# An FFT filter and a top-128 FFN: input rows laid out by halves on the host, and loaded by SyncE as 112 partitions and one

## The chip, the cores and the metric

One core of a Trainium2 chip runs the program. The time is device microseconds (us) of one execution. TensorE multiplies matrices into PSUM, VectorE and ScalarE work on SBUF and PSUM, GpSimd on SBUF alone, and SyncE (SP) issues DMAs. In the rows of the profile they are PE, DVE, ACT, POOL and SP; ACTq and SPq are the sequencers of ACT and SP, which hand out their instructions, DMA issues among them, in program order.

## What is computed

```
x: (8, 3136, 256) float32;  filt: (1569, 256), complex;  capacity C = 128
y   = irfft(rfft(x, axis=1) * filt, n=3136, axis=1)        # a filter along the sequence
s   = y . w_gate                                           # one score per row
top = the 128 rows of largest score, in each of 8 batches
out = y;  out[top] = y[top] + sigmoid(s[top]) * (relu(y[top] @ w1) @ w2)
```

## The kernel before

The transform of length 3136 = 98 * 32 is done by matmuls in two steps, and so is the way back.

**The work on one batch.** `outer` (by eight chunks of 32 channels) makes the first step of the batch that comes in and the last step of the batch that goes out. In: `fold` (L381) adds and subtracts the two halves of the rows, `amm` (L391) multiplies by the 98-point table, `tout` (L396) transposes into `UU`. A chunk that the plan names in `UNF` has no folds, and its `amm` has twice the matmuls ("plain"). Out: `tin` (L373) transposes from `UU`, `ymm` (L457) multiplies, `yout` (L460) copies from PSUM to `X`, and a store goes out once the four chunks of a half of the channels are done. `inner` (seven steps) does the 32-point part with the filter between: `zmm` (L292), `pmul` on VectorE (L300) and `zout` on ScalarE with `qmul` on GpSimd (L296, L303), `vmm` (L312), `vout` (L316, L320, L322), and the scores, `gate` on VectorE (L328) or `gmul` and `gsum` on GpSimd and ScalarE (L342, L347). `select` finds the 128 rows by counting (L604 on ScalarE, L613 on TensorE), after a trip of the scores through DRAM (`scr`, `R`, both DMAs on SP). While `inner` works on batch t, `outer` takes t-1 out and t+1 in. An FFN on the chosen rows ends the program.

**X** is one buffer for both ways: rows of y that wait for their store, and rows of x of the batch after next, by halves of the channels. A half is loaded when its store has read it, and stored when its chunks are done. A row of x is 256 channels in DRAM, so a half of it is a run of 512 bytes. The 49 rows of a quarter lie in a group of 64 partitions, the first 32 of them in order and the others at every second partition, and the rest of the group is set to zero at the start. A half takes ten DMAs: four on ACT's queue for one group, four on SP's for the other, and two on SP's for the last row of each. There are sixteen such loads in all.

**The order.** Each engine's order is made ahead of the run by a planner in the kernel: steps with a cost, what they read and write, and weights in `PLAN` (`LEAN`, `FOLD`, `UNF` and others). It replays the steps with these costs and always takes the one that could start first, after the weights. In that replay the ACT part of a load costs ACT 1.45, whatever its DMAs wait for:

```python
            op(when, "act", 1.45, lambda: rows_in(b, d, 1, nc.scalar), ["xpad"] if b == 0 else [], keys[1], lat=14.0 if b == 0 else 9.5, bias=bias)
            op(when + .001, "sp", 7.8, lambda: (rows_in(b, d, 0, nc.sync), last_in(b, d)), ["xpad"] if b == 0 else [], keys[0], lat=2.2, bias=bias)
```

On the chip the order within an engine is fixed, and semaphores alone hold it back. 160 warm-up matmuls on zeros (L987) stand first on TensorE.

Of the kernel before, what the change touches and what calls it, by code (L numbers as in the profile page):

```python
# [57 lines left out]
def _place():
    at = np.full(NH, LAST_ROW)
    for a, p, n, step in ROWS:  # L60
        at[a:a + n] = p + step * np.arange(n)
    return at


def _tables(C):
# [83 lines left out]
    TRING=['z', 'm', 'm', 'v', 'v'],
    URING=['v', 'm', 'v', 'z', 'm'],  # L150
# [3 lines left out]
    LEAN=dict(pmul=(-5.347, 0.016), yout=(-17.362, 0.336), turned=(38.666, -0.081), vhi=(-45.057, 1.291), gate=(4.527,  # L154
          1.5), vout=(17.794, -0.003), scatter=(-73.692, -0.615), tout=(-2.383, 0), zout=(14.722, 0.286), qmul=(0.524,
          0.201), tin=(39.462, -0.174), ymm=(-58.554, -0.011), vlo=(-25.455, -0.383), gather=(-40.475, 1.189), turn=(-6.285,
          0.267), xlo=(57.538, 0.676), yadd=(5.004, -0.444), swap=(24.566, 1.128), xhi=(-7.258, 1.5), amm=(8.954, 0.08),
          fold=(-24.881, -0.125), zmm=(-1.426, -0.093), vmm=(-1.82, -0.021), count=(-20.404, -0.51), total=(20.026, 0.066),
          over=(42.03, 0.547)),
    UNF=[[0, 1, 2, 3, 4, 7], [1, 2, 3, 6, 7], [], [0, 1], [0, 1], [0, 3, 4, 6], [0, 5], [0, 1]],  # L160
    GPOOL=[[1, 2, 3, 4, 5], [2, 3], [], [1, 2, 3, 5], [0, 1, 3, 5], [0, 2, 3, 4, 5], [1, 3, 4, 5], [0, 1, 3, 4]],
    JOIN=[[0, 1, 5, 7], [0, 2, 7, 8, 13]],
    IRING=['a'],
# [5 lines left out]
def kernel(  # L169
# [24 lines left out]
    xv = x.rearrange("b (h a g n) d -> b g a h n d", h=2, g=2, n=NG)  # L194
# [15 lines left out]
    X = const.tile([128, 2, NG, D], F32, name="X")  # L210
    XO = X.rearrange("p h n d -> p (h n) d")
# [54 lines left out]
    def inner(T0, TU, b):  # L266
# [5 lines left out]
        for i in range(NQ):  # L272
# [59 lines left out]
            op(t0, "pe", .49 * m + .02, zmm, [u for l in ls for u in row(b, l)] + ["tf"], new=Z, mode=1)  # L332
            op(t0 + 1.0, "act", .15 + .43 * m, zout, [Z], [Z], new=Q)
            op(t0 + 1.0, "dve", .12 + .54 * m, pmul, [Z, *(("fa", k) for k in parts)], new=Y)
            op(t0 + 2.0, "pool", 1.2 * m, qmul, [Q, *(("fb", k) for k in parts)], [Q])
            op(t0 + 4.5, "pe", .88 * m + .02, vmm, [Y, Q, "ti"], new=V, mode=1)
            op(t0 + 6.2, "act", .15 + .43 * m if n > 1 else .3, vout, [V], [V, *(u for l in ls for u in row(b, l))])
# [11 lines left out]
            for ks in ([0, 1], [2, 3]):  # L349
# [821 lines left out]
```

## Time and profile before

| | |
|---|---|
| Three runs | median 587.87 us (586.87 to 590.5) |
| The profiled execution | 585.63 us; its span from first to last instruction 583.8 us |
| Busy share of the span | PE 80%, DVE 70%, POOL 53%, ACT 49% |
| Mean granted TensorE clock | 0.904 of 2.4 GHz |
| DMA | 65.00 MB, mean 111 GB/s |

A busy share is a mean over stages: loading until the first filter product at 52.9 us, batch 0 alone until the first `tin` at 97.6, the first half of an output until its store at 126.2, then eleven half batches until the store at 467.3, and a tail with the last batches and the FFN. What bounds a stage is read from who waits for whom in it.

### The profile page before, as it was taken

Reading aid. Unit: us, or ns where it says so; the run is one execution under the profiler, and the core shown is the slowest. Engines: PE = TensorE matmul, PEld = TensorE weight load, DVE = VectorE, ACT = ScalarE, POOL = GpSimd, SP = SyncE. Lnnn points to the kernel's source line nnn. Section 1 sums busy time; section 2 is a strip of 40 time slices with the busy share of each in tenths; the row PEclk is TensorE's granted clock in tenths of the full one; section 3 lists DMA queues with packets and bytes.
Section 4 is the critical chain, followed back from the end, with each engine's and each line's share of the span. In section 5 each row is a group of like instructions: output and inputs, shape, how many; then the busy total and the mean of one; then the engine's idle time right before and its main releaser. Section 6 shows DMA issues by size and latency. Waiting matters only on the chain.

```text
span 583.8 us, 11344 instructions
## 1 busy us (share of the span) xinstructions
PE 469.4 (80%) x4268; PEld 244.6 (42%) x4268; DVE 411.0 (70%) x988; ACT 284.6 (49%) x612; POOL 312.1 (53%) x202
## 2 busy tenths in 40 slices
PE   9932859899969695997689586969878987869996
PEld 9611424343423242432244132424432354546996
DVE  6443855899949584895579485857859799887542
ACT  1211632586436342784267144545365688936421
POOL 5342976893727151862455053546536389973422
PEclk9985988999979797998989797989978999968999
DMA  9998062328562647045913635180653166513521
GB/s 198 242 230 166 1 111 64 79 61 162 149 112 78 144 113 138 10 136 119 199 21 105 134 113 121 32 190 3 168 84 112 29 185 170 116 44 88 120 70 37
DMA packets 110157, 65.00 MB, mean 111 GB/s; under 512 B 5014, under 2 KB 108438, under 8 KB 109846
## 3 DMA queue, kind: packets, MB, share of 16 engines
q1 hardware_dynamic: 83734, 49.59, 35.3%
q10 hardware_dynamic: 25600, 12.59, 11.5%
q0 software_dynamic: 768, 2.10, 1.2%
q8 instruction: 34, 0.56, 0.4%
q14 instruction: 21, 0.17, 0.1%
HBM read 37.34 MB, written 26.91 MB: 110 GB/s over the span
## 4 chain that ended last, share of the span: by engine, by line
PE 45%; DMA 22%; POOL 8%; DVE 8%; issue 8%; ACT 6%; SPq 1%; ACTq 1%; POOLq 0%; DVEq 0%
DMA X<-in_x_dram 13%; PE py L457 13%; PE pv L312 10%; PE pa L391 8%; DMA out_dram<-X 5%; PE pz L292 5%; POOL q L303 3%; POOL X L429 2%; ACT X L460 2%; PE pa L420 2%; PE pa L898 1%; PE pv L865 1%; DVE X L381 1%; POOL xl L342 1%; DMA fb_sb<-in_fri_dram 1%
## 5 line engine op out<-in xcount | busy, mean ns | idle before, releaser
L303 POOL TENSOR_TENSOR q<-q,fb_sb 128x1024 f32<-128x1024 f32 (+1 forms) x56 | 125.1, 2234 | 171.2 <-ACT q L296 146.9
L457 PE MATMUL py<-t,c_sb 128*98 128x512 f32 x192 | 114.0, 678 | 33.2 <-ACT X L460 32.5
L460 ACT COPY X<-py 98x512 f32<-98x512 f32 x96 | 56.1, 584 | 86.6 <-DMA X<-in_x_dram 46.3
L300 DVE TENSOR_TENSOR y<-pz,fa_sb 128x1024 f32<-128x1024 f32 (+1 forms) x56 | 63.6, 1137 | 44.9 <-ACT q L296 28.4
L391 PE MATMUL pa<-X,c_sb 64*64 64x512 f32 x464 | 89.0, 636 | 1.0 <-DVE UU L396 1.0
L396 DVE STREAM_TRANSPOSE UU<-pa 128x1024 f32<-128x1024 f32 x59 | 73.2, 1241 | 18.9 <-PE pa L391 18.6
L292 PE MATMUL pz<-UU,tf_sb 64*64 64x256 f32 x800 | 62.8, 410 | 26.5 <-DVE y L300 24.6
L373 DVE STREAM_TRANSPOSE t<-UU 128x1024 f32<-128x1024 f32 x64 | 78.8, 1231 | 5.7 <-PE py L457 3.2
L328 DVE SCALAR_TENSOR_TENSOR rj<-pv,wg_sb 128x256 bf16<-128x256 f32 x144 | 60.1, 417 | 27.1 <-ACT UU L320 14.7
L312 PE MATMUL pv<-y,ti_sb 64*64 64x256 f32 x800 | 70.0, 405 | 7.6 <-DVE rj L328 6.2
L296 ACT COPY q<-pz 128x1024 f32<-128x1024 f32 (+1 forms) x56 | 53.2, 949 | 30.8 <-PE pz L292 14.3
L312 PE MATMUL pv<-q,ti_sb 64*64 64x256 f32 x800 | 67.3, 391 | 0.0
L292 PEld LDWEIGHTS pz<-UU,tf_sb 64*64 64x64 f32 x800 | 29.9, 137 | 65.3 <-DVE y L300 30.1
L457 PEld LDWEIGHTS py<-t,c_sb 128*98 128x98 f32 x192 | 25.6, 175 | 70.1 <-ACT X L460 51.5
L342 POOL TENSOR_TENSOR xl<-UU,wg_sb 128x512 f32<-128x512 f32 x28 | 37.7, 1348 | 29.2 <-ACT UU L320 20.8
L391 PE MATMUL pa<-xh,c_sb 64*64 64x512 f32 x160 | 52.2, 716 | 1.1 <-DVE UU L396 0.6
L312 PEld LDWEIGHTS pv<-y,ti_sb 64*64 64x64 f32 x800 | 31.1, 140 | 44.7 <-issue 13.6
L381 POOL TENSOR_TENSOR xh<-X 128x512 f32<-128x512 f32 x28 | 38.1, 1367 | 21.1 <-DMA tf_sb<-in_tf_dram 15.7
L613 PE MATMUL pm<-cr_sb,cnt 128*128 128x16 f32 x56 | 21.8, 389 | 30.1 <-ACT junk L604 29.7
L312 PEld LDWEIGHTS pv<-q,ti_sb 64*64 64x64 f32 x800 | 34.9, 140 | 13.7 <-issue 2.5
L381 POOL TENSOR_TENSOR X<-X 128x512 f32<-128x512 f32 x28 | 38.7, 1389 | 2.1 <-DVE xh L381 1.4
L320 ACT COPY UU<-pv 128x1024 f32<-128x1024 f32 x24 | 24.2, 1007 | 31.4 <-PE pv L312 21.7
(207 smaller groups left out, 745.0 us busy)
## 6 DMA issues: line engine op xcount, KB each, us to landing
out_dram<-X SPq DMA_DIRECT2D x12, 1568.0 KB
X<-in_x_dram ACTq DMA_DIRECT2D x32, 256.0 KB
X<-in_x_dram SPq DMA_DIRECT2D x32, 256.0 KB
out_dram<-X SPq DMA_DIRECT2D x16, 384.0 KB
X<-in_x_dram SPq DMA_DIRECT2D x32, 128.0 KB
X<-in_x_dram ACTq DMA_DIRECT2D x32, 128.0 KB
R<-scr SPq DMA_DIRECT2D x14, 196.0 KB
fb_sb<-in_moe_w_dram SPq DMA_DIRECT2D x2, 1024.0 KB
```

The costliest lines, as they stand in the source:

```text
L292: nc.tensor.matmul(z[o, hi, e], lhsT=tf_sb[p, l], rhs=urow(b, l, 0, D)[p], start=True, stop=True)
L296: nc.scalar.copy(out=wide(q), in_=wide(h["z"]))
L300: nc.vector.tensor_tensor(out=wide(y), in0=wide(h["z"]), in1=filt(fa_sb), op=ALU.mult)
L303: nc.gpsimd.tensor_tensor(out=wide(h["q"]), in0=wide(h["q"]), in1=filt(fb_sb), op=ALU.mult)
L312: nc.tensor.matmul(v[o, j, c], lhsT=ti_at[p, k, 2 * i + e, hi], rhs=y[p, hi, c], start=k == 0, stop=k == 1)
L328: nc.vector.scalar_tensor_tensor(out=rj, in0=h["v"][:, k % 2, k // 2 * D:k // 2 * D + D], scalar=1.0, in1=wg_sb, op0=ALU.mult, op1=ALU.mul ...
L373: nc.vector.transpose(out=h["t"].rearrange("p d (l j) -> p d l j", j=2), in_=uchan(b_out, c))
L381: eng.tensor_tensor(out=area(1) if k else h["f"], in0=area(0), in1=area(1), op=(ALU.add, ALU.subtract)[k])
L391: nc.tensor.matmul(ap[64 * k:64 * k + 64, g].rearrange("p (n d) -> p n d", d=DW), lhsT=todo[k][i][0][p], rhs=todo[k][i][1][p], start=i == ...
L396: nc.vector.transpose(out=uchan(b_in, c), in_=a.rearrange("p (l j) d -> p d l j", j=2))
L457: nc.tensor.matmul(yp[:N1], lhsT=cc["wi"], rhs=half(), start=True, stop=True)
L460: nc.scalar.copy(out=XO[:N1, :, q * CW:(q + 1) * CW], in_=h["y", k][:N1])
```

## The change

The host lays x out anew: by batch, then by half of the channels, then 113 rows of 16 KB (49 rows of one quarter, 15 of zeros, 49 of the other), so that a partition's share of a half is one run in DRAM and, with `X` stored by halves too, one in SBUF. A load is two DMAs on SP's queue, 112 rows and the last one; ACT issues none. The zeroing of `X` at the start falls away, folds take 113 partitions, and `amm` 49 rows of a group. Bytes of a load go from 1568 KB to 1808 KB. A store is still one DMA with runs of 512 bytes in DRAM.

```diff
-    X = const.tile([128, 2, NG, D], F32, name="X")
-    XO = X.rearrange("p h n d -> p (h n) d")
+    X = const.tile([128, 2, 2, NG, HD], F32, name="X")
+    XO = X.rearrange("p x h n d -> p x (h n) d")
...
-                eng.tensor_tensor(out=area(1) if k else h["f"], in0=area(0), in1=area(1), op=(ALU.add, ALU.subtract)[k])
+                eng.tensor_tensor(out=(area(1) if k else h["f"])[:64 + NH], in0=area(0)[:64 + NH], in1=area(1)[:64 + NH],
+                                  op=(ALU.add, ALU.subtract)[k])
...
-                            p = slice(64 * g, 64 * g + 64)
+                            p = slice(64 * g, 64 * g + NH)
...
         if b < B:
-            keys = [[("x", h, c, g) for c in range(h * n, h * n + n)] for g in range(2)]
-            op(when, "act", 1.45, lambda: rows_in(b, d, 1, nc.scalar), ["xpad"] if b == 0 else [], keys[1], lat=14.0 if b == 0 else 9.5, bias=bias)
-            op(when + .001, "sp", 7.8, lambda: (rows_in(b, d, 0, nc.sync), last_in(b, d)), ["xpad"] if b == 0 else [], keys[0], lat=2.2, bias=bias)
+            keys = [("x", h, c, g) for c in range(h * n, h * n + n) for g in range(2)]
+            to = X[:, h].rearrange("p k n d -> p (k n d)")
+
+            def fetch():
+                nc.sync.dma_start(out=to[:112], in_=x[b, h, :112])
+                nc.sync.dma_start(out=to[112:64 + NH], in_=x[b, h, 112:])
+
+            op(when, "sp", 7.2, fetch, [], keys, lat=2.2, bias=bias, tag="load")
...
-    for g, k, e in ((0, 0, "dve"), (0, 1, "pool"), (1, 0, "dve"), (1, 1, "pool")):
-        op(-99.9 + .01 * g, e, 3.5, lambda g=g, k=k, e=e: dict(dve=nc.vector, pool=nc.gpsimd)[e].memset(X[32 + 64 * g:64 + 64 * g, k], 0.0), (), ["xpad"])
...
-    data = {k: np.ascontiguousarray(inputs[k]) for k in ("x", "moe_w_gate", "moe_w1", "moe_w2")}
+    data = {k: np.ascontiguousarray(inputs[k]) for k in ("moe_w_gate", "moe_w1", "moe_w2")}
+    rows_of = np.asarray(inputs["x"]).reshape(B, 2, NH, 2, NG, 2, D // 2).transpose(0, 5, 3, 2, 1, 4, 6)
+    data["x"] = np.zeros((B, 2, 64 + NH, S * D // (4 * NH)), np.float32)
+    data["x"][:, :, :NH], data["x"][:, :, 64:] = rows_of.reshape(B, 2, 2, NH, -1).transpose(2, 0, 1, 3, 4)
```

The planner has new costs for most steps, a replay that charges TensorE's steps double while it takes the clock to be low, and a new table `PLAN`, so that nearly every row of every engine's order moves. Of the table:

```diff
-    AO6=0.179, AO7=0.099, SD=-34.762, WARM=160, FR=17.139, F0=-30.458, G7=-25.255, INV=2,
+    AO6=0.353, AO7=0.107, SD=-30.114, WARM=85, FR=12.002, F0=-84.921, G7=-79.774, INV=2,
```

Counted over the program: warm-up matmuls 160, then 85; folds on VectorE 26, then 36, and on GpSimd 56, then 48; plain chunks 23, then 22 (of batches 2 to 7 12, then 14); score products on VectorE 144, then 152, on GpSimd 28, then 24; the counting steps of one batch more (batch 4) end on ScalarE instead of VectorE.

The order on three places. First ACT at the start of the program, before: loads of batches 0 and 1 (L481) ahead of the copies of the filter table (L966) and the first `zout` (L296).

```order
L481 DMA X<-in_x_dram 32x16x128 x2
L481 DMA X<-in_x_dram 16x16x128 x2
L995 ACTIVATE ti_sb<-ti_sb 32x1664 x2
L481 DMA X<-in_x_dram 32x16x128 x2
L481 DMA X<-in_x_dram 16x16x128 x2
L966 COPY fb_sb<-fb_sb 32x1024 x2
L481 DMA X<-in_x_dram 32x16x128 x2
L481 DMA X<-in_x_dram 16x16x128 x2
L296 COPY q<-pz 128x1024 x2
```

The same place of the changed kernel, where L950 is the copy of the table, L979 the turn of `ti_sb` and L285 `zout`:

```order
L983 ACT_TABLE_LOAD
L983 ACTIVATE sc<-ge 128x1
L950 COPY fb_sb<-fb_sb 32x1024
L979 ACTIVATE ti_sb<-ti_sb 32x1664
L285 COPY q<-pz 128x1024
L979 ACTIVATE ti_sb<-ti_sb 32x1664
```

No DMA stands ahead of the first `zout` now. VectorE at this place, before, up to the first `pmul` (L300):

```order
L396 STREAM_TRANSPOSE UU<-pa 128x32x16x2
L396 STREAM_TRANSPOSE UU<-pz 128x32x16x2
L396 STREAM_TRANSPOSE UU<-pv 128x32x16x2
L396 STREAM_TRANSPOSE UU<-pa 128x32x16x2
L396 STREAM_TRANSPOSE UU<-pz 128x32x16x2
L966 COPY fa_sb<-fa_sb 32x2048
L300 TENSOR_TENSOR y<-pz,fa_sb 128x1024
```

And in the changed kernel, up to its first `pmul` (L289):

```order
L386 STREAM_TRANSPOSE UU<-pa 128x32x16x2
L977 COPY ti_sb<-ti_sb 32x1664
L386 STREAM_TRANSPOSE UU<-pz 128x32x16x2
L962 CAST cr_sb<-UU 128x16
L950 COPY fa_sb<-fa_sb 32x1024
L977 COPY ti_sb<-ti_sb 32x1664
L950 COPY fb_sb<-fb_sb 32x2048
L289 TENSOR_TENSOR y<-pz,fa_sb 128x1024
```

Ahead of them stand six of the eight transposes and all seven folds of batch 0 on VectorE; the turns of `ti_sb`, which stood before all transposes, have come in between.

Second, ACT in the stage of half batches, before: the load between a `yout` (L460) and the next one, with a count of `select` (L604) behind it.

```order
L460 COPY X<-py 98x32x16
L481 DMA X<-in_x_dram 32x16x128 x2
L481 DMA X<-in_x_dram 16x16x128 x2
L460 COPY X<-py 98x32x16
L604 ACTIVATE junk,cnt<-R,c_sb 128x392
L296 COPY q<-pz 128x1024
L322 COPY UU<-pv 128x2x512
```

The changed kernel at the first count of the same batch (L588 is the count, L450 `yout`, L311 `vout`):

```order
L285 COPY q<-pz 128x1024
L311 COPY UU<-pv 128x2x512
L450 COPY X<-py 98x32x16
L588 ACTIVATE junk,cnt<-R,c_sb 128x392
L285 COPY q<-pz 128x1024
L450 COPY X<-py 98x32x16
L611 ACTIVATE ok,J<-pm,c_sb 128x15
L612 ACTIVATE nb<-J,nd 128x1
```

The computing rows are of the same kinds, and nothing that waits for a store is among them.

Third, SP in the same stage, before: a store (L469), its load, the next store, `select`'s trip through DRAM (L548, L574) and that store's load.

```order
L469 DMA out_dram<-X 3136x1x128
L481 DMA X<-in_x_dram 32x16x128 x2
L481 DMA X<-in_x_dram 16x16x128 x2
L486 DMA X<-in_x_dram 2x16x128 x2
L469 DMA out_dram<-X 3136x1x128
L548 DMA scr<-kf 98x2x32
L574 DMA R<-scr 128x1x392 x2
L481 DMA X<-in_x_dram 32x16x128 x2
L481 DMA X<-in_x_dram 16x16x128 x2
L486 DMA X<-in_x_dram 2x16x128 x2
```

And the changed kernel (L459 the store, L475 and L476 the load, L532 and L558 the trip):

```order
L459 DMA out_dram<-X 3136x1x128
L475 DMA X<-in_x_dram 112x4096
L476 DMA X<-in_x_dram 1x4096
L459 DMA out_dram<-X 3136x1x128
L532 DMA scr<-kf 98x2x32
L558 DMA R<-scr 128x1x392 x2
L475 DMA X<-in_x_dram 112x4096
L476 DMA X<-in_x_dram 1x4096
```

SP keeps the sequence store, trip, load; six issues of a load have become two, and four on ACT none.

## Rows read from the trace of the kernel before

**Rows 1.** Waits of ACT: engine, line, waited for, us in total, times, longest.

```profile
ACT X L460 <- DMA X<-in_x_dram: 46.3, 7, 9.9
...
ACT fb_sb L966 <- DMA X<-in_x_dram: 22.3, 1, 22.3
...
ACT Dt L522 <- DMA X<-in_x_dram: 5.9, 1, 5.9
```

**Rows 2.** Waits of PE.

```profile
PE py L457 <- ACT X L460: 32.5, 16, 6.6
PE pm L613 <- ACT junk L604: 29.7, 6, 7.8
PE pz L292 <- DVE y L300: 24.6, 2, 18.3
```

**Rows 3.** Timeline, SP and ACT, 205 to 236 us: start, us, what.

```profile
210.17 0.93 SPq L469 DMA_DIRECT2D out_dram<-X  x1
...
219.28 9.28 ACTq L481 DMA_DIRECT2D X<-in_x_dram  x4
228.60 0.58 ACT L460 COPY X<-py 98x512 f32<-98x512 f32 x1 [9.94 <-DMA X<-in_x_dram]
```

**Rows 4.** Timeline of PE behind it; in brackets its wait and what ended it.

```profile
229.85 0.38 PE L613 MATMUL pm<-cr_sb,cnt 128*128 128x16 f32 x1 [7.23 <-ACT junk L604]
```

**Rows 5.** Stages: length; busy us (count) of PE, PEld, DVE, ACT, POOL; clock, DMA, GB/s.

```profile
52.90:97.60 44.70, 34.35 (x388) 17.79 (x388) 30.95 (x52) 19.94 (x35) 34.28 (x20) 0.82 0.25 47
97.60:126.20 28.60, 25.99 (x254) 11.63 (x250) 24.54 (x59) 15.97 (x28) 25.09 (x18) 1.00 0.32 73
126.20:467.30 341.10, 278.59 (x2373) 116.80 (x2373) 252.68 (x657) 176.52 (x385) 163.60 (x97) 0.90 0.47 108
467.30:583.80 116.50, 96.97 (x825) 73.70 (x817) 80.73 (x207) 64.39 (x159) 71.10 (x54) 0.94 0.39 104
225.70:235.90 10.20, 6.05 (x28) 2.15 (x29) 4.30 (x7) 5.84 (x13) 4.30 (x3) 0.50 0.53 83
```

**Rows 6.** The same for ten stretches without a long gap, and their sum.

```profile
103.70:160.10 56.40, 54.98 (x552) 24.40 (x552) 53.44 (x151) 35.14 (x63) 40.75 (x25) 1.00 0.48 109
...
sum 246.20, PE 239.69 PEld 105.83 DVE 220.94 ACT 145.26 POOL 159.42; mean PE 23.97 PEld 10.58 DVE 22.09 ACT 14.53 POOL 15.94
```

**Rows 7.** Timeline of the start, PE, ACT and DVE.

```profile
1.00 20.15 PE L987 MATMUL pm<-ge 128*64 128x64 f32 x320 [1.00 <-POOL ge L237]
...
31.64 9.83 ACTq L481 DMA_DIRECT2D X<-in_x_dram  x4
...
45.81 5.96 ACTq L481 DMA_DIRECT2D X<-in_x_dram  x4
51.81 1.01 ACT L296 COPY q<-pz 128x1024 f32<-128x1024 f32 x1 [8.21 <-DMA X<-in_x_dram]
...
52.91 1.23 DVE L300 TENSOR_TENSOR y<-pz,fa_sb 128x1024 f32<-128x1024 f32 x1 [16.38 <-issue]
```

**Rows 8.** DMA rates (last column) of three stretches of the start.

```profile
2.00:5.00 3.00, 3.00 (x40) 3.00 (x39) 3.00 (x1) 0.24 (x2) 2.94 (x2) 1.00 0.83 302
...
8.00:14.00 6.00, 6.00 (x107) 6.00 (x106) 3.56 (x3) 0.00 (x0) 0.07 (x1) 1.00 1.10 195
...
20.00:25.00 5.00, 5.00 (x57) 2.45 (x59) 1.87 (x2) 0.00 (x0) 1.25 (x1) 1.00 1.03 276
```

**Rows 9.** Groups of DVE instructions: us busy, mean ns of one.

```profile
L396 DVE STREAM_TRANSPOSE UU<-pa 128x1024 f32<-128x1024 f32 x43 | 53.4, 1243 | 6.4 <-PE pa L391 6.0
...
L328 DVE SCALAR_TENSOR_TENSOR rj<-pv,wg_sb 128x256 bf16<-128x256 f32 x102 | 42.5, 417 | 17.6 <-ACT UU L320 9.2 <-ACT UU L316 4.3 <-ACT UU L322 2.1
...
L966 DVE COPY fb_sb<-fb_sb 32x2048 f32<-32x2048 f32 x2 | 3.4, 1718 | 0.1
```

**Rows 10.** Folds on DVE: ns min/median/max.

```profile
L381 DVE TENSOR_TENSOR xh<-X x13: 651/909/1742, 24.4 to 402.8; 128x512 f32<-128x512 f32 x13
L381 DVE TENSOR_TENSOR X<-X x13: 644/1449/4875, 26.7 to 442.1; 128x512 f32<-128x512 f32 x13
```

More of the change, by code (lines that the diff above doesn't have):

```diff
@@ L153 @@
     BUFS=dict(z=1, a=1, v=1, y=1, m=1, xh=2, xl=1, t=2, q=2, yt=2, hh=2),
[L154 to L163, printed above, removed]
+    LEAN=dict(pmul=(-17.833, 0.025), yout=(1.726, 0.154), turned=(23.986, 0.021), gate=(16.381, 1.166), vout=(36.271,
+          0.066), scatter=(-67.841, -0.939), tout=(-13.222, 0.007), zout=(9.289, 0.236), qmul=(-0.511, 0.365), tin=(52.691,
+          -0.133), ymm=(-59.95, 0.015), gather=(-38.113, 1.397), turn=(-4.89, 1.257), amm=(3.373, 0.077), fold=(-25.967,
+          -0.67), zmm=(-25.886, -0.181), vmm=(8.041, -0.068), count=(5.896, -0.64), total=(12.215, 0.019), over=(67.926,
+          0.566), fold0=(5.465, -0.026), fold1=(5.322, -0.025), join=(-0.599, 0.046), imm=(-25.208, 0.069), iout=(-2.545,
+          1.5), gmul=(7.498, 0.012), gsum=(-2.837, -0.018), load=(0.551, 0), store=(3.228, 0.416)),
+    UNF=[[3, 5, 7], [0, 3, 4, 6, 7], [0, 4], [0, 6], [7], [0, 4, 6], [0, 6, 7], [1, 3, 7]],
+    GPOOL=[[0, 2, 4, 5], [2, 3, 4, 5], [0, 2, 3], [0, 2], [3, 5], [0, 3], [0, 3, 4, 5], [0, 1, 3]],
+    JOIN=[[1, 2, 4, 7, 13, 15], [3, 4, 14]],
+    IRING=['a', 'a'],
     HRING=['a', 'z', 'v'],
@@ L331, in inner @@
             parts = sorted({part_of[2 * i + e] for e in range(m)})
[L332 to L335, printed above, removed]
+            op(t0, "pe", .49 * m + .04, zmm, [u for l in ls for u in row(b, l)] + ["tf"], new=Z, mode=1)
+            op(t0 + 1.0, "act", .09 + .43 * m, zout, [Z], [Z], new=Q)
+            op(t0 + 1.0, "dve", .08 + .535 * m, pmul, [Z, *(("fa", k) for k in parts)], new=Y)
+            op(t0 + 2.0, "pool", .1 + 1.13 * m, qmul, [Q, *(("fb", k) for k in parts)], [Q])
             op(t0 + 4.5, "pe", .88 * m + .02, vmm, [Y, Q, "ti"], new=V, mode=1)
-            op(t0 + 6.2, "act", .15 + .43 * m if n > 1 else .3, vout, [V], [V, *(u for l in ls for u in row(b, l))])
+            op(t0 + 6.2, "act", .09 + .43 * m if n > 1 else .3, vout, [V], [V, *(u for l in ls for u in row(b, l))])
             def gmul(h=h, i=i):
@@ L457, in ymm, with yout @@
                     nc.tensor.matmul(yp[:N1], lhsT=cc["wi"], rhs=half(), start=True, stop=True)
-                def yout(h=h, k=k, q=q):
-                    nc.scalar.copy(out=XO[:N1, :, q * CW:(q + 1) * CW], in_=h["y", k][:N1])
-                op(t1 + 2.5, "pe", .90, ymm, [T_, "c"], new=PY_)
-                op(t1 + 3.3, "act", .52, yout, [PY_], XS[2 * k:2 * k + 2])
+                def yout(h=h, k=k, q=q, hx=hx):
+                    nc.scalar.copy(out=XO[:N1, hx, :, q * CW - hx * HD:(q + 1) * CW - hx * HD], in_=h["y", k][:N1])
@@ L464, in outer @@
+                op(t1 + 2.5, "pe", .95, ymm, [T_, "c"], new=PY_)
+                op(t1 + 3.3, "act", .50, yout, [PY_], XS[2 * k:2 * k + 2])
             if c * DW + DW in (HD, D):
-                op(t0 + TC + 3.4, "sp", 7.7, lambda f=store, hx=hx: f(b_out, hx, xy),
-                   [("x", hx, q, g) for q in range(hx * NCH // 2, (hx + 1) * NCH // 2) for g in range(2)], [("out", b_out)], lat=.9)
+                op(t0 + TC + 3.4, "sp", 6.8, lambda f=store, hx=hx: f(b_out, hx, xy),
+                   [("x", hx, q, g) for q in range(hx * NCH // 2, (hx + 1) * NCH // 2) for g in range(2)], [("out", b_out)], lat=.9, tag="store")
@@ L1092 @@
     place_of, seen, pemode = {}, {}, 0
-    free["sp"] = 11.0
+    win, acc, cold = 0, 0.0, 0.0
+    free["sp"] = 1.0
     for n, p in enumerate(prog):
@@ L1130 @@
         cost += WAIT[e] * max(0, len(need) - 1)
+        if e == "pe":
+            while (win + 1) * WIN <= t:
+                if acc < LOW * WIN:
+                    cold = (win + 3) * WIN
+                win, acc = win + 1, 0.0
+            if t < cold:
+                cost = 2 * cost if t + 2 * cost <= cold else cost + (cold - t) / 2
+            u, v = t, t + cost
+            while (win + 1) * WIN <= v:
+                acc += (win + 1) * WIN - u
+                u = (win + 1) * WIN
+                if acc < LOW * WIN:
+                    cold = (win + 3) * WIN
+                win, acc = win + 1, 0.0
+            acc += v - u
         free[e] = done[n] = t + cost
```

85 lines of the change are left out of this document (35 added, 50 removed).

## The prediction, made before the change was run

> **What bounds the kernel now.** I read the waits first, then the stages, then one wait in the order of time. ACT stands idle behind its own issue of X loads: seven rows from [rows 1] (the first, the second and the last are shown), 127.5 us in 15 waits. PE's longest waits are for ACT's `yout` and counts, and one for VectorE's first filter product [rows 2]. How they hang together is seen at 210: the store of a half goes out at 210.17, ACT reaches the load of that half, can issue it only when the store has read X, and is busy issuing until 228.6; a `yout`, a count, a `zout` and a `vout` stand behind it on ACT [rows 3], and PE waits 7.23 us for the count [rows 4]. So the loads cost through the queue on which they stand, not through their bytes.
>
> The stages [rows 5]: the eleven half batches from 126.2 to 467.3 take 341.1 us, in which PE is idle for 62.5, and the clock column says 0.90: a fifth of it, 68 us, at 1.2 GHz instead of 2.4. The low stretches begin in a gap and outlast it: of the 10.2 us from 225.7 PE worked 6.05, the rest was the end of its wait. Between the gaps PE is busy for 97.4% and VectorE for 89.7% of ten stretches, 246.2 us in sum [rows 6]. So two engines are nearly full when ACT isn't held. In the start VectorE waits 16.38 us for the first `pmul` at 52.91, and ACT's two groups of issues, 9.83 and 5.96 us long, stand ahead of the first `zout` at 51.81 [rows 7].
>
> The profiled execution took 585.63 us, 1.8 more than its span, and 2.2 less than the median of the runs shown. The sum is made on its span.
>
> **The change part by part.**
>
> *Loads on ACT go.* All 64 issues of ACT fall away, with the waits of [rows 1]. SP keeps two issues of a load where it had six, in the same sequence of store, load, `select`'s trip. Its load waits for the store as before; behind it on SP stand the trip's two steps and the next store, as before, so nobody waits anew.
>
> *The load itself.* 1808 KB instead of 1568, but in runs of 16 KB. Rates at the start [rows 8]: 302 GB/s while runs of 6.6 KB moved, 276 with mixed tables, 195 while x moved in runs of 512 bytes. No row shows 16 KB; I take 302, the nearest, which gives 6.1 us, and keep 195 (9.5 us) as the other end. A turn of a half is then about 9.1 us of store (210.17 to ACT's issue at 219.28 [rows 3]), 6.1 of load and an estimated 2 of issue and landing: 17 us, 21 at the low rate. It has to fit beside the work on the other half, 25.8 us by the sum below, so it lies hidden with 5 to 9 us to spare. If that cover went, every us late would cost one, eleven times.
>
> The Trainium skill, DMA: Bandwidth & Descriptors, section on why a DMA increments its semaphore by 16, says that a DMA is spread over the largest number of engines up to 16 that divides its outer size: 16 for 112 rows, one for 113. No run here shows it; by it the sum stands as it is, and the last rival below is unlikely.
>
> *Zeroing, 113 partitions, 49 rows.* Nothing: the zeroing ran while x was on its way, and folds and `amm` keep their 512 columns a partition, whichever rows take part.
>
> *The start.* c_sb and the first half are 1.95 MB, 6.5 us at 302 GB/s from about 2 us on; with 1 us for landing VectorE begins at 9.5 (the 85 warm-up matmuls end at 1 + 20.15 x 85/160 = 11.7, beside its first folds [rows 7]). Until the first `pmul` it has 7 folds of 0.909 [rows 10], 8 transposes of 1.243 and four copies of 32 partitions, 1664, 1024, 1664 and 2048 long, at 1.718 for 2048 [rows 9]: 6.4 + 9.9 + 5.4 = 21.7. First `pmul` at 31.2 instead of 52.9. Tables that must be there by then bring the bytes to 7.1 MB, 28 us at 276 GB/s. Bounds: 28 with the shortest folds (0.65) and shorter copies, 40 if all comes at 195 GB/s.
>
> *Batch 0 alone,* first `pmul` to first `tin`, 44.7 before. VectorE had 30.95 us of work [rows 5]; it gets a transpose (1.2), three folds at 1.18 (mean of the two medians [rows 10]), two score products at 0.5 with their read (0.417 and an estimated 0.08) and half a table copy: 37.5. At the 89.7% of [rows 6] that is 41.8; 38 without waits, 46 with as many as before. First `tin` at 73.
>
> *First half of an output.* 28.6 before, at full clock and with PE at 91% [rows 5]; I keep it, 25 to 31.
>
> *Eleven half batches.* Two prices, and the greater holds. PE: 278.6 busy, less what the low clock doubled (68 x 6.05/10.2 = 40 us of work, so 20), plus two plain chunks more of 16 records at 278.6/2373 = 0.117 each (3.8): 262.4, at 97.4% 269 us. VectorE: 252.7, three folds more (3.5), four score products more (2.0), eight counting steps fewer at about 0.42 (3.4): 254.8, at 89.7% 284 us, or 51.6 a batch instead of 62. I take 284. Where the gaps go, VectorE is late next; PE is 15 us behind it. It is not a floor that VectorE has shown, since in a run without gaps it may be fuller than 89.7%, or less full if PE's order waits on it: at 85.8%, as from 97.6 to 126.2, it is 297. So 269 to 305, with some for the new order.
>
> *The tail* from the last store of these has no load in it (the half batches took them all). 116.5 is kept; the new order may win or lose the half of its stretch at 1.2 GHz (clock 0.94, 14 us): 110 to 123.
>
> Sum: 73 + 28.6 + 284 + 116.5 + 1.8 = 503.9. Brought to the median of the runs shown (587.87/585.63): **506 us**, 82 less than now: 25 from the start, 57 from the half batches.
>
> **The rivals.**
>
> *TensorE alone sets the half batches.* VectorE gets full enough that 269 holds: 73 + 28.6 + 269 + 116.5 + 1.8 = 489, 491 by the median. For it: some short stretches have VectorE at 95% (53.44 of 56.4 [rows 6]). Against: each engine's order is fixed, and 97% and 95% at once leave no slack.
>
> *Folds that wait for GpSimd.* Ten more folds go to VectorE. A fold there has taken from 0.644 to 4.875 us for one size [rows 10], so something holds it. If the 24 in the half batches took the middle between the longer median and the longest, 3.16, that is 2.0 each more: (254.8 + 48)/0.897 = 338, and 560 in all. The trace speaks against it: one median is 0.909. The Trainium skill, SBUF — State Buffer, section on the two separate sides, says that a VectorE operation with two SBUF inputs and a GpSimd operation lock each other out for a whole instruction; the spread of [rows 10] agrees, the medians show that it is not paid each time.
>
> *The wait changes queue.* SP now holds the whole load behind the store and behind a trip whose scores come late; x lands late and PE waits for `amm`. With half of the idle time and the low clock left (62.5 + 20, halved) it is 41 more: 547. For it: less slack, 25.8 us a half instead of 31. Against: the turn is no longer than before.
>
> *It doesn't do what it says.* ACT is free, but the half batches still take 341 because the counts and `yout` came late for another reason: 73 + 28.6 + 341.1 + 116.5 + 1.8 = 561, 563 by the median.
>
> *Slower.* The 16 KB runs are served by few DMA engines. A half batch is then 9.1 us plus the load; the kernel is slower than 585.6 from 11 half batches of 33.3, a load of 24 us, 76 GB/s, a quarter of 302. At that rate the three loads of the start after the first cost 18 more each, and it ends at about 645. Against: 6.6 KB runs reached 302 on the same queue.
>
> **How the numbers follow.** Forecast 0.59, TensorE alone 0.14, folds 0.08, changed queue 0.10, no effect 0.05, slower 0.04. The range takes in the first, the second and the fourth, and the bounds of the terms: their distances below and above add in squares to about 17 and 24. From the second case less 17 to just over the fourth: 474 to 548, with 0.17 outside by the rivals. One per cent, 5.9 us, is about what a measurement of this kernel can tell from no change. All cases but the last are faster by more: faster 0.95, same 0.01, slower 0.04.
>
> **What the profile of the changed kernel would show.** No row of ACT behind X<-in_x_dram. First `pmul` near 31, first `tin` near 73, first store near 102. Stores of a half about 26 apart, PE's clock at 0.97 or above from the first to the twelfth, VectorE near 90% busy there. A load of 112 rows lands 7 to 9 us from its issue. The prediction is wrong if PE has gaps over 2 us before `amm` (changed queue), if folds on VectorE lie over 2 us in the mean, if VectorE passes 94% with PE at 97% (too high), or if tables or the second half of x hold the start past 40.

## The result, and the profile after

| | kernel before | changed kernel |
|---|---|---|
| median of the runs | 587.67 us (586.87 to 590.5, 4 runs) | 527.43 us (524.97 to 533.46, 4 runs) |
| span of the profiled execution | 583.8 us | 523.2 us |

The ratio is 0.8953, 95% interval 0.8891 to 0.9016: 60 us less, where 82 were forecast, and inside the range. The ratio leaves out the changed kernel's run of 533.46 us, which is 1.6% above its fastest and counts as slow; the other three are 524.97 to 529.37 us. The stages of the changed kernel, beside [rows 5] (length; busy us of PE, PEld, DVE, ACT, POOL; clock, DMA, GB/s):

```profile
37.50:80.20 42.70, 35.26 (x396) 18.23 (x400) 35.04 (x59) 24.64 (x33) 30.64 (x18) 0.89 0.59 152
80.20:110.70 30.50, 26.91 (x268) 11.31 (x264) 26.71 (x71) 17.21 (x33) 17.77 (x10) 1.00 0.23 64
110.70:415.80 305.10, 276.88 (x2439) 116.32 (x2435) 254.00 (x654) 182.50 (x408) 166.52 (x99) 0.96 0.47 129
415.80:523.20 107.40, 90.36 (x753) 67.89 (x745) 71.09 (x191) 58.58 (x144) 61.74 (x49) 0.98 0.43 113
```

The eleven half batches, the third row, took 36 us less than before, not 57. PE's idle time there fell from 62.5 to 28.2 us. ACT has no row behind X any more, so [rows 1] are gone. Its longest wait on a DMA in that stretch is a new one, for the trip's second part, and PE's longest wait is for the count behind it; PE hardly waits for x. PE's waits from 110.7 to 415.8:

```profile
PE pm L597 <- ACT junk L588: 14.8, 5, 6.4
PE pz L281 <- DVE y L289: 3.2, 3, 2.0
PE py L447 <- ACT X L450: 2.9, 5, 0.7
PE pa L381 <- DMA X<-in_x_dram: 1.3, 2, 0.7
```

The longest of them is shown in the order of time. The trip is the way of `select`'s 98 rows of `kf` to DRAM (scr) and, spread over 128 partitions, back (R):

```profile
137.33 0.93 SPq L459 DMA_DIRECT2D out_dram<-X  x1
...
139.54 0.22 DVE L528 CAST kf<-pm 98x64 f32<-98x64 int32 x1
139.79 3.64 SPq L532 DMA_DIRECT2D scr<-kf  x1
...
146.62 1.23 SPq L558 DMA_DIRECT2D R<-scr  x2
147.96 0.52 SPq L475 DMA_DIRECT2D X<-in_x_dram  x1
...
150.89 0.62 ACT L588 ACTIVATE junk<-R,c_sb 128x392 bf16<-128x392 f32 x1 [6.89 <-DMA R<-scr]
...
151.66 0.38 PE L597 MATMUL pm<-cr_sb,cnt 128*128 128x16 f32 x1 [6.40 <-ACT junk L588]
```

A store went out on SP 2.5 us ahead of the trip. The trip's first issue takes 3.64 us where the one at 246, with no store near, takes 0.33, R is asked for at 146.62, and the first count stands on ACT until 150.89. Then PE's clock falls: the stretches of this stage at 1.2 GHz, of which the first begins in that gap, hold 23.66 us of PE's work, so 11.8 us were lost to them (two of five rows, and their sum):

```profile
149.60:156.43 6.83, 4.77 (x23) 1.89 (x27) 3.28 (x13) 3.46 (x7) 0.00 (x0) 0.50 1.04 266
...
252.00:258.83 6.83, 6.09 (x40) 2.98 (x44) 4.95 (x19) 5.05 (x11) 3.31 (x2) 0.50 0.41 113
...
sum 27.26, PE 23.66 PEld 9.99 DVE 17.98 ACT 13.52 POOL 13.44; mean PE 4.73 PEld 2.00 DVE 3.60 ACT 2.70 POOL 2.69
```

In the start the first half of x is there at 11.63 and the second at 20.82; PE runs dry for 3.22 us before the second, and the first `pmul` is at 37.50, where [rows 7] have 52.91:

```profile
11.63 0.69 DVE L370 TENSOR_TENSOR xh<-X 113x512 f32<-113x512 f32 x1 [11.63 <-DMA X<-in_x_dram]
...
20.82 0.69 DVE L370 TENSOR_TENSOR xh<-X 113x512 f32<-113x512 f32 x1 [1.77 <-DMA X<-in_x_dram]
...
22.68 1.38 PE L381 MATMUL pz<-xh,c_sb 49*64 49x512 f32 x2 [3.22 <-POOL xh L370]
```

### The profile page after: what moved, and what is told of

Its sections match the earlier page's. It is cut to its first block, busy times and chain, and to the rows that moved or that the text cites. A ratio compares the mean times of both kernels' runs of the same rounds, so it can differ in the third digit from the quotient of the medians.

```text
span 523.2 us, 10675 instructions
## 1 busy us (share of the span) xinstructions
PE 458.2 (88%) x4110; PEld 231.1 (44%) x4110; DVE 406.2 (78%) x990; ACT 288.8 (55%) x622; POOL 284.3 (54%) x184
## 4 chain that ended last, share of the span: by engine, by line
PE 37%; DMA 30%; DVE 16%; ACT 8%; POOL 4%; issue 4%; SPq 0%; POOLq 0%; ACTq 0%; DVEq 0%
DMA X<-in_x_dram 13%; PE pv L301 10%; PE py L447 9%; PE pa L381 5%; PE pz L281 5%; DMA out_dram<-X 4%; DMA scr<-kf 4%; DMA R<-scr 4%; DMA fb_sb<-in_fri_dram 3%; DVE rj L317 3%; DVE UU L386 3%; DVE y L289 2%; DVE t L362 2%; ACT q L285 1%; DVE X L370 1%
## 5 line engine op out<-in xcount | busy, mean ns | idle before, releaser
L447 PE MATMUL py<-t,c_sb 128*98 128x512 f32 x192 | 108.5, 648 | 3.0 <-ACT X L450 2.9
L381 PE MATMUL pa<-X,c_sb 49*64 49x512 f32 x476 | 84.3, 609 | 2.6 <-DMA X<-in_x_dram 1.3
L317 DVE SCALAR_TENSOR_TENSOR rj<-pv,wg_sb 128x256 bf16<-128x256 f32 x152 | 63.8, 420 | 22.7 <-ACT UU L309 10.1
L450 ACT COPY X<-py 98x512 f32<-98x512 f32 x96 | 55.8, 581 | 38.7 <-PE py L447 33.5
L289 DVE TENSOR_TENSOR y<-pz,fa_sb 128x1024 f32<-128x1024 f32 (+1 forms) x56 | 63.4, 1132 | 13.9 <-ACT q L285 13.8
L281 PE MATMUL pz<-UU,tf_sb 64*64 64x256 f32 x800 | 64.7, 421 | 9.7 <-DVE y L289 7.0
L285 ACT COPY q<-pz 128x1024 f32<-128x1024 f32 (+1 forms) x56 | 53.0, 946 | 19.9 <-PE pz L281 18.6
L370 POOL TENSOR_TENSOR xh<-X 113x512 f32<-113x512 f32 x24 | 33.4, 1395 | 50.6 <-DMA X<-in_x_dram 19.0
L381 PE MATMUL pa<-xh,c_sb 49*64 49x512 f32 x156 | 48.9, 633 | 4.1 <-DVE UU L386 3.0
L331 POOL TENSOR_TENSOR xl<-UU,wg_sb 128x512 f32<-128x512 f32 x24 | 33.8, 1409 | 26.3 <-ACT UU L309 15.6
L447 PEld LDWEIGHTS py<-t,c_sb 128*98 128x98 f32 x192 | 24.5, 168 | 39.5 <-ACT X L450 16.6
L597 PE MATMUL pm<-cr_sb,cnt 128*128 128x16 f32 x56 | 20.9, 373 | 18.0 <-ACT junk L588 17.9
L588 ACT ACTIVATE junk<-R,nb 128x392 bf16<-128x392 f32 (+1 forms) x48 | 30.0, 626 | 11.9 <-DVE nb L607 11.2
```

The source lines that it names most:

```text
L281: nc.tensor.matmul(z[o, hi, e], lhsT=tf_sb[p, l], rhs=urow(b, l, 0, D)[p], start=True, stop=True)
L285: nc.scalar.copy(out=wide(q), in_=wide(h["z"]))
L289: nc.vector.tensor_tensor(out=wide(y), in0=wide(h["z"]), in1=filt(fa_sb), op=ALU.mult)
L317: nc.vector.scalar_tensor_tensor(out=rj, in0=h["v"][:, k % 2, k // 2 * D:k // 2 * D + D], scalar=1.0, in1=wg_sb, op0=ALU.mult, op1=ALU.mul ...
L370: eng.tensor_tensor(out=(area(1) if k else h["f"])[:64 + NH], in0=area(0)[:64 + NH], in1=area(1)[:64 + NH], op=(ALU.add, ALU.subtract)[k])
L381: nc.tensor.matmul(ap[64 * k:64 * k + 64, g].rearrange("p (n d) -> p n d", d=DW), lhsT=todo[k][i][0][p], rhs=todo[k][i][1][p], start=i == ...
```

## The experiments: what set ScalarE free

The change has three parts: who issues the loads, how long their runs are, and the table behind the order. "The changed order" is that of the changed kernel, "the old order" that of the kernel before, word for word on PE.

**e1, the queue alone.** In the kernel before, the line that issues group 1 from ScalarE:

```diff
-            op(when, "act", 1.45, lambda: rows_in(b, d, 1, nc.scalar), ["xpad"] if b == 0 else [], keys[1], lat=14.0 if b == 0 else 9.5, bias=bias)
+            op(when, "act", 1.45, lambda: rows_in(b, d, 1, nc.sync), ["xpad"] if b == 0 else [], keys[1], lat=14.0 if b == 0 else 9.5, bias=bias)
```

> The kernel before, with ACT's part of each load issued by SP; order, table, layout and runs of 512 bytes stay. Theory (ACT's queue): the ten long gaps of TensorE (54 us) and most of the low clock (20) go, a little comes back as VectorE gets late: 520 to 550. Rival (longer runs in DRAM make the gain) and rival (the new order makes it): 580 to 595, as before.

526.63 us (521.69 to 526.85), ratio 0.8935 [0.8872, 0.8998]: the whole gain from one word. In its half batches TensorE waits 17.9 us for `yout` and the counts, where the kernel before has 60.3:

```profile
119.10:407.20 288.10, 265.25 (x2371) 113.10 (x2371) 251.00 (x657) 176.71 (x385) 163.60 (x97) 0.98 0.60 128
```

**e2, the loads back on ScalarE.** In the changed kernel:

```diff
-                nc.sync.dma_start(out=to[:112], in_=x[b, h, :112])
-                nc.sync.dma_start(out=to[112:64 + NH], in_=x[b, h, 112:])
+                nc.scalar.dma_start(out=to[:112], in_=x[b, h, :112])
+                nc.scalar.dma_start(out=to[112:64 + NH], in_=x[b, h, 112:])
```

> The changed kernel, with its two DMAs of a load issued by ACT; layout, table and the order of all computing stay. Theory (ACT's queue): ACT stands behind stores again, 5 to 9 us a half batch, 560 to 590. Rivals (longer runs, or the new order): 520 to 535, as the changed kernel.

530.41 us (529.52 to 533.22), 0.9034 [0.8979, 0.9089]: a miss by 30 us. The two issues hold ACT for 0.62 us where [rows 3] have 9.28:

```profile
123.12 0.32 ACTq L475 DMA_DIRECT2D X<-in_x_dram  x1
123.47 0.30 ACTq L476 DMA_DIRECT2D X<-in_x_dram  x1
```

ACT now waits for the store alone, 4.8 us in three waits of the half batches. So the place on its queue does not hold it by itself. What the 9.28 us of [rows 3] are is in the trace of the kernel before. That row merges four issues, from the start of the first to the end of the last; all 64 issues of ACT, one by one (ns, least/median/most), are short:

```profile
L481 ACTq DMA_DIRECT2D X<-in_x_dram x64: 317/584/811, 1.0 to 425.3; - x64
```

Between them ACT waits for other DMAs to land. The last of the four follows a load of SP's, as the chain that ended last from 217 to 230 us has it (start, us, what):

```profile
221.35 6.60 DMA X<-in_x_dram
227.96 0.02 issue
227.98 0.58 ACTq L481
228.60 0.10 ACT X L460
```

The records of the issues name the semaphores that tell of a landing. Eight serve the DMAs of SP and ACT in turn, and 51 of ACT's 64 issues wait until the DMA that had their semaphore before has landed. The second of the four issues waits so for R's first part, which landed at 223.98, the third and fourth for two of SP's issues of a load, at 226.35 and 227.96; the four take 1.8 us themselves. Over the program ACT's 64 issues take 33 us and its waits at them 96, of which 88 end with an earlier DMA's landing and 3 with a store's. With ten DMAs in a load the semaphore's last user is still on its way; with two (e2) or three (e10) no such wait is left in the half batches. Their many short packets are not shown to matter: e7 below issues 3136 packets of 512 bytes from ACT as one DMA, in 0.85 us. No run changed the number of DMAs alone. Either remedy, the other queue or few DMAs, frees ACT.

**e3, the runs back to 512 bytes.** The changed kernel with x as the host has it, six DMAs a half on SP, and the zeroing of rows 49 to 63:

```diff
...
+                        nc.sync.dma_start(out=X[64 * g:64 * g + 48, h, k], in_=xv[b, g, :48, k, :, d])
+                    nc.sync.dma_start(out=X[48:64 + NH:64, h, k], in_=xv[b, :, 48, k, :, d])
...
```

> The changed kernel with x as the host had it: SP loads a half in six DMAs with runs of 512 bytes, and 32 partitions are zeroed once; the order stays. Theory (loads lie hidden once they are off ACT): 525 to 537, the start later by a few us and the half batches the same within 5. Rival (longer runs make the gain): 550 or more.

564.44 us (563.05 to 566.43), 0.9611 [0.9556, 0.9665], also a miss. Its start is 9.8 us longer than the changed kernel's, the stretch from there to the first store 6.7 and the half batches 22.0. In these, 327.1 us, TensorE waits 9.4 us in 4 for x and 7.3 in 2 for GpSimd's fold, which waits for x in turn. In the changed order x is late when its loads take the time of short runs; in the old one (e1) it isn't.

**e9 and e10, the long runs in the old order.** The kernel before with x by halves and padded rows; a half is loaded as 64, 48 and 1 rows at the two places of the old loads, in e9 all from SyncE, in e10 rows 64 to 112 from ScalarE. The zeroing stays, so the first load goes out at 9.6 us in e9.

```diff
...
+        if g:
+            eng.dma_start(out=to[64:112], in_=x[b, h, 64:112])
+            eng.dma_start(out=to[112:64 + NH], in_=x[b, h, 112:])
+        else:
+            eng.dma_start(out=to[:64], in_=x[b, h, :64])
...
```

> The kernel before with nothing changed in the order of TensorE's instructions: x by halves and padded rows, X by halves, and all of a half's loads, now three DMAs of 64, 48 and 1 rows of 16 KB, from SyncE in the two places where the old loads stood. Beside it stands the run with the old order and the old 512-byte loads on SyncE, 526.6 us. Theory (with SyncE issuing, the old order hides the slow loads already; the long runs help the start alone): the start 44 to 38 us, half batches 280 to 290, together 512 to 524. Rival 1 (the long runs are worth in the old order what they were worth in the new one, 37 us): under 500. Rival 2 (they are worth nothing, or the trip through DRAM meets packets of 16 KB on the engines): 525 to 540.

> The run above, but rows 64 to 112 of a half issued from ScalarE, as group 1 was before the change: the long runs and nothing else. Theory (many packets, not the queue, held ScalarE): two DMAs of 49 packets hold it for 0.6 us, no wait of ScalarE behind X, and the time is that of the run above or up to 10 us more. Rival 1 (the queue counts whatever the packets): 560 to 590. Rival 2 (the trip through DRAM, on SyncE, no longer stands in one queue with a load and meets its packets on the engines, as with the trip on ScalarE): 15 to 30 us above the run above, with the wait of ScalarE behind R over 40 us.

e9: 551.59 us (550.49 to 551.74), 0.9405 [0.9369, 0.9441], 25 us above e1 and above all that was expected. e10: 560.30 (559.21 to 562.78), 0.9564 [0.9523, 0.9605]: the long runs, and with them three DMAs a half in the place of ten, are worth 27 us with ScalarE still issuing. As its theory had it, no wait of ScalarE behind X stands in its list and the time is 9 us above e9; rival 2's wait for R is there too, 42.6 us in six. Beside e1, e9 loses 12 us up to the first store, with the late first load, and 15 in the half batches. Two things differ there, and no run parts them. The load is slower than the changed kernel's, 172 GB/s while it is in flight:

```profile
142.00:150.00 8.00, 8.00 (x72) 3.44 (x73) 7.69 (x33) 4.20 (x9) 1.47 (x2) 1.00 1.01 172
```

against 277 in the changed kernel, whose load is one DMA of 112 rows:

```profile
121.50:127.00 5.50, 5.50 (x62) 2.78 (x58) 4.77 (x13) 3.08 (x7) 1.75 (x3) 1.00 1.01 277
```

The runs' length is the same in both; but in e9 rows 0 to 63 and rows 64 to 111 move one after the other, and land at 147.4 and 152.8. The Trainium skill, SBUF — State Buffer, section on the DMA port swizzle, says that partitions 0 to 63 reach only half of the memory's 16 DMA ports. The two rows agree with it; no run here changed the split alone. And the old order has a load right ahead of the trip on SP, so that scr's packets stand behind a load's:

```profile
162.45 0.27 SPq L478 DMA_DIRECT2D X<-in_x_dram  x1
162.75 0.33 SPq L541 DMA_DIRECT2D scr<-kf  x1
175.04 1.20 SPq L567 DMA_DIRECT2D R<-scr  x2
```

12.3 us between the trip's two issues, where e1 has 6.2 at the same place.

**e5 and e6, the old table in the changed kernel,** with the loads on SyncE and on ScalarE. All of PLAN is the old one.

> The changed kernel with the table of numbers of the kernel before: long runs and SyncE's queue stay, the order of the instructions goes back towards the old one. Theory (the new order is what holds the half batches at 305.1 us: with the old order and the loads on SyncE they took 288.1, while its start and tail were 6.6 and 10.2 us longer): start 38 to 44, up to the first store 75 more, half batches 284 to 292, tail 117, together 515 to 526 us. Rival 1 (the order is worth nothing in the half batches, the long runs and the trip through DRAM set them): half batches about 305 and the tail about 117, together 535 to 545. Rival 2 (the new order is worth what the changed kernel gained over the queue alone elsewhere, and the old order loses with loads of this size): over 545.

> The run above with the two load DMAs of a half issued from ScalarE. Theory (ScalarE was held in the kernel before because many short packets of a load filled its queue; two DMAs of 113 long packets never do, 0.6 us of ScalarE a half): within 6 us of the run above, and no wait of ScalarE behind X in its table of waits. Rival (with the old order ScalarE's queue is what counts, whatever the packets): 545 to 585 us, with the wait of ScalarE behind X of 20 us or more.

587.74 us (580.11 to 590.27), 0.9958 [0.9856, 1.0059], and 615.41 (612.80 to 618.65), 1.0510 [1.0437, 1.0582]. The theory of e5 fell, with half batches of 316.7 us and a tail of 148.6 for 288 and 117, because the old numbers in the new code give a third order, not the old one. In e6 the tail is 147.5 us, with TensorE waiting 16.7, 8.0 and 7.3 us for rows that the FFN gathers. What the new table is worth against the old order can't be read from this pair. e6 misses too, 28 us above e5. Its half batches are as much longer, 344.1, and its rows point to the trip: ACT waits 48.9 us for R in seven waits, e5 25.8, and at 162 and 225 a load went out on ACT's queue just before R on SP's.

## The experiments: the trip

**e4, the trip from ScalarE.** Both of its issues (lines 532 and 558), all else as changed:

```diff
-            nc.sync.dma_start(out=scr.rearrange("t (a c) -> a t c", c=N2), in_=st["kf"])
+            nc.scalar.dma_start(out=scr.rearrange("t (a c) -> a t c", c=N2), in_=st["kf"])
...
```

> The changed kernel with the two steps of the scores' trip through DRAM issued by ACT, so that they stand behind no store in SP's queue; all other orders stay. Theory (what is left in the half batches is that the trip waits behind a store): ACT's 23.8 us of waits for R shrink, TensorE's gaps before the counts too, 508 to 520. Rival (ACT then waits for the trip's own steps instead): 525 to 545.

557.51 us (556.83 to 563.46), 0.9513 [0.9439, 0.9588]: 30 us slower than the changed kernel, a miss that taught most. The same trip as above:

```profile
141.41 0.34 ACTq L532 DMA_DIRECT2D scr<-kf  x1
144.72 0.33 SPq L475 DMA_DIRECT2D X<-in_x_dram  x1
145.11 0.27 SPq L476 DMA_DIRECT2D X<-in_x_dram  x1
145.36 1.21 ACTq L558 DMA_DIRECT2D R<-scr  x2
155.33 0.62 ACT L588 ACTIVATE junk<-R,c_sb 128x392 bf16<-128x392 f32 x1 [12.48 <-DMA R<-scr]
```

The issue is short now, but nothing holds the load back: it goes out 0.6 us before R, whose 256 packets of 1568 bytes then travel among 113 of 16 KB and land 10 us after their issue, not 4. So it is in all seven trips: R's first part took 9.9 to 10.4 us in the four that met a load and 2.9 to 3.2 in the three that met none. A queue of its own took the trip's place ahead of the load away. In the half batches ACT's wait for R grew from 23.8 to 52.9 us, and the stage from 305.1 to 339.3, with TensorE's wait for the counts up from 14.8 to 42.1: the order has too little to put beside the trip.

**e7 and e8, the store from ScalarE,** in the changed kernel and in e5. Its last writer is ACT itself, so ACT needn't wait to issue it.

```diff
-        nc.sync.dma_start(out=ov[b, :, :, h * HD:(h + 1) * HD], in_=XO[:N1, h])
+        nc.scalar.dma_start(out=ov[b, :, :, h * HD:(h + 1) * HD], in_=XO[:N1, h])
```

> The changed kernel with the half batch's store issued from ScalarE, so that the trip of the selection's bits to DRAM and back is no longer queued behind 3136 packets of a store on SyncE. Theory (that queue is what makes TensorE wait before line 597: 12.3 us in three gaps, and the low clock behind them): the issue of the trip's first DMA falls from 3.6, 2.0 and 1.5 us to under 0.5, those gaps to under 4 us in all, half batches 290 to 300, 510 to 522 us. Rival 1 (the packets share the 16 DMA engines with the store's wherever they are queued): the gaps stay, 524 to 531. Rival 2 (the store's packets fill ScalarE's queue and hold its copies as the loads did): ScalarE waits behind the store, over 535.

> The changed kernel with the old table and the half batch's store issued from ScalarE: both edits together. Theory (they add): 5 to 10 us under the run with the old table alone, 507 to 518 us if that one gives 515 to 526. Rival 1 (the old order has the trip elsewhere and gets nothing from it): within 3 us of that run. Rival 2 (the store holds ScalarE): 10 us or more above it.

520.74 us (517.84 to 523.03), 0.8888 [0.8828, 0.8948], and 581.56 (578.66 to 587.82), 0.9912 [0.9836, 0.9989]: e7's median is 6.7 us under the changed kernel's, though the intervals of the two ratios touch; e8's runs overlap e5's, so nothing is shown there. The 3136 packets of a store hold ACT for 0.85 us, so the second rival of e7 is out. The first trip again:

```profile
136.29 0.85 ACTq L459 DMA_DIRECT2D out_dram<-X  x1
138.79 0.33 SPq L532 DMA_DIRECT2D scr<-kf  x1
144.18 1.16 SPq L558 DMA_DIRECT2D R<-scr  x2
...
147.32 0.62 ACT L588 ACTIVATE junk<-R,c_sb 128x392 bf16<-128x392 f32 x1 [4.33 <-DMA R<-scr]
```

The issue is down to 0.33 us as expected, but R is asked for 5.4 us later all the same, with the store's packets still on the way. The three gaps before the counts fell from 12.3 to 8.7 us, not under 4; the store ahead in the queue was three tenths of them, and the rest is put down to the trip's own length and the order, which e7 does not part. The half batches missed too: 303.9 us, not 290 to 300, with 3.7 us less lost to the low clock and no less idle time.

**e12, the plan is told how long the trip takes.** e7's kernel, with the trip as one step of SyncE:

```diff
-            step(T0 + 2.2, "sp", .2, s6, lat=LS)
-            step(T0 + 5, "sp", 2.0, s7, (), [("R", 0)], lat=LS)
+            step(T0 + 2.2, "sp", 5.5, lambda: (s6(), s7()), (), [("R", 0)], lat=1)
```

> The changed kernel with its stores on ScalarE, and with the trip of the selection's bits given to the plan as one step of SyncE of 5.5 us that lands 1 us later, where the table said that R is there 15.5 us before it is asked for; everything else in the table is kept, and the plan orders all engines anew. Theory (a trip takes 6 us or more and the order leaves nothing beside it, which is 12 us of gaps before the counts and the low clock behind them): gaps before the counts under 4 us in the half batches, TensorE's clock 0.97 or above there, half batches 280 to 295, together 500 to 515. Rival 1 (the other numbers of the table were found for the order without the trip, and the counts that come later hold the next selection): 525 to 550, with gaps in other places. Rival 2 (the gaps were hidden behind VectorE anyway): within 4 us of the run with the stores on ScalarE, 520.7.

512.68 us (512.26 to 515.92), 0.8748 [0.8696, 0.8801], below the interval of the changed kernel and of e1: the theory held in every number. The tail, 116.0 us for 107.9 in e7, gave back some of the gain. The half batches of e12 and what is left there at 1.2 GHz:

```profile
106.10:395.20 289.10, 267.10 (x2430) 113.31 (x2424) 251.54 (x655) 182.31 (x410) 162.63 (x98) 0.99 0.49 136
...
sum 3.41, PE 3.25 PEld 1.61 DVE 2.82 ACT 1.62 POOL 0.73; mean PE 3.25 PEld 1.61 DVE 2.82 ACT 1.62 POOL 0.73
```

PE's longest waits in that stretch:

```profile
PE py L447 <- ACT X L450: 7.0, 11, 1.4
...
PE pm L596 <- ACT junk L587: 2.2, 3, 1.2
```

No gap of PE is over 2 us. Split by what PE did in the half batches (its work with the low clock's half taken off, the time lost to that clock, and its idle time):

| | half batches | work | low clock | idle |
|---|---|---|---|---|
| before | 341.1 | 254.6 | 24.0 | 62.5 |
| e1 | 288.1 | 258.8 | 6.5 | 22.9 |
| changed kernel | 305.1 | 265.1 | 11.8 | 28.2 |
| e4 | 339.3 | 265.1 | 17.6 | 56.6 |
| e7 | 303.9 | 267.0 | 8.1 | 28.8 |
| e12 | 289.1 | 265.5 | 1.6 | 22.0 |

The changed kernel, e4 and e12 do the same work, and between the changed kernel and e12 lie 16.4 us of idle time and low clock. The plan of e12 orders everything anew, so this isn't the trip's price to the us; but the gaps that are gone are those before the counts.

## One DMA for all 113 rows

```diff
-                nc.sync.dma_start(out=to[:112], in_=x[b, h, :112])
-                nc.sync.dma_start(out=to[112:64 + NH], in_=x[b, h, 112:])
+                nc.sync.dma_start(out=to[:64 + NH], in_=x[b, h, :64 + NH])
```

> The changed kernel with a half loaded by one DMA of 113 rows in the place of 112 and 1. Theory of the rival that was put at 645 us (113 rows don't divide among 16 DMA engines, so few engines carry them): loads of 1.85 MB at a fraction of the 257 to 265 GB/s, TensorE waits for X, 600 us or more. Other theory (113 packets of 16 KB are shared as 8 and 7 to an engine either way): within 5 us of the changed kernel.

1486.83 us in the one run that there is. From 250 to 300 us nothing but a load is in flight; the DMA column is 0.06, one engine of 16, at 27 GB/s:

```profile
250.00:300.00 50.00, 0.00 (x0) 0.00 (x0) 0.00 (x0) 0.00 (x0) 0.00 (x0) 0.51 0.06 27
```

and GpSimd alone waits half of the span for x:

```profile
POOL xh L370 <- DMA X<-in_x_dram: 740.3, 12, 74.3
```

By the Trainium skill, DMA: Bandwidth & Descriptors, section on why a DMA increments its semaphore by 16, which the prediction could only cite, 113 rows go to one engine. The trace agrees. The last rival, put at 645 us, was thus a real danger and far dearer than its price, and it is the row apart in a DMA of its own that keeps the changed kernel clear of it.

## Why the prediction was right, and where its size was off

*Loads on ACT go.* Right, and e1 shows that this step alone is the gain. "Not through their bytes" holds; "through the queue on which they stand" was half of it. ACT was not "busy issuing until 228.6": its four issues took 1.8 us, and the rest were waits for other DMAs to land, because a load was ten DMAs. e2 and e10 leave loads on ACT as two DMAs, and ACT is not held.

*The load itself.* 302 GB/s were taken, 277 measured. Issued at 119.47, its first fold is at 129.44; 10 us instead of 7 to 9. It is hidden as forecast but for 1.3 us of PE's waits in the stage.

*The start.* 37.5 instead of 31.2, within its bounds of 28 to 40. VectorE began at 11.63 instead of 9.5, and the second half of x came at 20.8; after the 3.22 us in which PE waited for its fold the clock was 1.2 GHz, from 23.31 to 30.14.

*Batch 0 and the first half.* 42.7 and 30.5 us instead of 41.8 and 28.6.

*Eleven half batches.* The term that was mis-sized: 305.1 instead of 284. Both amounts of work were right, VectorE's at 254.8 (254.0 measured) and PE's at 262.4 (265.1). What failed is the share, 89.7% of VectorE, taken from stretches without gaps; it had 83.2%. Behind that is one sentence, that the trip's steps stand behind the load "as before, so nobody waits anew". In the sequence of SP it was true; but ACT had been too late for its counts itself, and with ACT free the trip became what ends last. e4 (longer trip, the stage up by 34) and e12 (counts moved away from it, 289.1 us) show it; e7 (store out of its way) took 3.6 us off the gaps but 1.2 off the stage. With e12 VectorE stands at 87% and PE's gaps are gone, 5 us from the forecast of this term.

*The tail.* 107.4 instead of 116.5, a gain that the prediction had left to the new order, and larger than its bound of 110.

The differences are 6.3 + 0.9 + 1.9 + 21.1 - 9.1 = 21.1 us of span. That the total came so near is in part luck: without the tail's 9.1 us, for which the prediction had no reason, it would have missed by 30.

*The rivals.* Folds on VectorE took 1.03 and 1.18 us in the mean, so GpSimd didn't hold them for long. TensorE alone did not set the stage, in e12 neither. The changed queue, as it was put, x late before `amm`, did not come; what came is its neighbour on the same queue. Its sign, a gap over 2 us before `amm`, stands once in the changed kernel, in the start (3.22 us); in the half batches PE's longest wait for x is 0.7. The reason of the rival that it does nothing, counts late for something other than ACT, came true for the 14.8 us of PE's waits for them. e1, without the new layout and table, gives the same time as the whole change, so these two added nothing in sum. With SyncE issuing, the old order took 526.6 us with short runs (e1) and 551.6 with long ones in three DMAs (e9), the new order 564.4 with short runs (e3) and 527.4 with long ones: each alone cost time, and together they cost none. The old order with a half in one DMA of 112 rows was not run.

## What to carry to other kernels

A DMA issue on a compute engine's queue is cheap, 0.3 to 1.0 us here (3.64 for the trip's, 2.5 us behind a store's 3136 packets in its queue). When it must wait, for its data or for an earlier DMA that had its semaphore, every instruction behind it waits. So look at each issue's own duration and at what ended the wait before it, since a merged row hides both, and make fewer DMAs of many or give them to an engine with nothing else to do. When a wait is removed, ask for each remaining round trip what stands beside it: here the next one was a trip through DRAM of 5 to 11 us that the plan believed free, and telling the plan its length, with all else ordered anew, was worth 8 us on top of clearing its queue. A queue also keeps an order: taking a small urgent transfer off the queue of a large one may put it behind the large one.

## What had not been expected of the hardware

- The issues that held ScalarE were themselves short, 0.32 to 0.81 us. What held it were waits for earlier DMAs with the same semaphore, eight semaphores in turn for loads of ten DMAs: 88 us over the kernel before.
- A transfer in a second queue is not served ahead of one that was issued just before it elsewhere: R took 10 us beside a load of 16 KB packets (e4), and 3 to 4 when both stood in SP's queue with R first (changed kernel).
- Packets of 16 KB moved at 277 GB/s as one DMA of 112 partitions and at 172 as DMAs of 64 and 48 (e9).
- One outer size that has no divisor but itself, 113, cost 960 us in 16 loads (e11, one run).
